# A linear-attention and mixer kernel on one core: own PSUM tiles for the fifth products, and the last outputs on another DMA queue

## The chip, the core and the metric

The kernel runs on one core of a Trainium2 chip. A core has a matrix engine (TensorE, PE), a vector engine (VectorE, DVE), a scalar engine (ScalarE, ACT), a general engine (GpSimd, POOL) and a synchronising engine (SyncE, SP). Each has its own stream of instructions, and they wait for each other through semaphores. PE writes its results into PSUM, from which DVE and ACT read them. Transfers between SBUF and the memory outside are started by SP, ACT or POOL and carried out by 16 DMA engines. The metric is the time of one execution in microseconds (us); lower is better. The kernel before took 264.2 us, the median of three runs (263.92 to 264.7).

## The reference

Eight batches of 576 rows. An attention without softmax makes x of each batch (576 x 512); a mixer over the rows and then one over the channels make the output.

```python
q_p, k_p = (phi(q), phi(k))                       # phi(x) = where(x > 0, x, exp(x) - 1) + 1
kv  = np.einsum('bhsd,bhse->bhde', k_p, v)
z   = np.sum(k_p, axis=2)
num = np.einsum('bhsd,bhde->bhse', q_p, kv)
den = np.einsum('bhsd,bhd->bhs', q_p, z)[..., None] + 1e-06
x   = num / den                                   # heads side by side: 8 x 576 x 512
# ... the mixer
h   = np.maximum(xt @ w_tok1, 0.0) @ w_tok2       # xt: rows and columns of x exchanged
u   = x + h.transpose(0, 2, 1)
h2  = np.maximum(u @ w_ch1, 0.0) @ w_ch2          # 512 -> 1536 -> 512
return (u + h2).astype(np.float32)
```

## The kernel before

The batches are numbered n = 0 to 7 and follow each other in a pipeline. For each batch, `mm3` multiplies u with w_ch1 in 12 tiles (c_ps, line 480), ACT applies the maximum with zero (cr, line 487), and a last product with w_ch2 gives the output. In batches 0 to 5 that last product is done directly (`mm4`, line 506). In batches 6 and 7 it is done by Strassen's scheme in Winograd's form: 512 of the 576 rows and the channels are cut into blocks of two by two, and seven block products take the place of eight. There are two pairs of row tiles, j = 0 and 1, so 14 products of six matmuls each per batch.

```python
ps_big = ctx.enter_context(tc.tile_pool(name="ps_big", bufs=4, space=bass.MemoryType.PSUM))
ps_sm = ctx.enter_context(tc.tile_pool(name="ps_sm", bufs=2, space=bass.MemoryType.PSUM))
outp = ctx.enter_context(tc.tile_pool(name="outp", bufs=5))
# ...
def product(n, j, i):
    b, p = n % 2, n // 2
    a_ = lambda h, e: ablock(n, h, e)[:, :, j]
    lhs, rhs, tile_, first = {
        1: (a_(0, 0), wblock(0, 0), "X", True), 2: (a_(1, 0), wblock(1, 0), "Z", True),
        6: (sb[1][:, :, j], tb[1], "X", False), 5: (sb[0][:, :, j], tb[0], "Y", True),
        7: (sb[2][:, :, j], tb[2], "X", False), 4: (a_(1, 1), tb[3], "X", False),
        3: (sb[3][:, :, j], wblock(1, 1), "Y", False)}[i]
    if first and tile_ != "Y":
        live[tile_, j] = ps_big.tile([128, 512], FP32, name="h2_ps", tag="big")[:, 0:256]
    elif first and j == 0:
        t = ps_sm.tile([128, 2, 512], FP32, name="y_ps", tag="sm")
        live["Y", 0], live["Y", 1] = t[:, 0, 0:256], t[:, 1, 0:256]
    ps = live[tile_, j]
    for k_ in range(KH):                                         # KH = 6; line 606
        nc.tensor.matmul(out=ps, lhsT=lhs[:, k_], rhs=rhs[:, k_], start=(first and k_ == 0),
                         stop=(k_ == KH - 1), skip_group_check=not first)
    if i == 1:
        live["oj", j] = outp.tile([128, 2, DM], FP32, name="o_sb", tag="o_sb")
    o = live["oj", j]
    ur = lambda e, c: u[b][:, 2 * j + e, HC[c]]
    add = lambda e, c, x_, y_: nc.vector.tensor_tensor(out=o[:, e, HC[c]], in0=x_, in1=y_,
                                                       op=ALU.add)   # line 612
    if i == 1:
        add(0, 0, ps, ur(0, 0))
    elif i == 2:
        add(0, 0, ps, o[:, 0, HC[0]])
    elif i == 6:
        add(0, 1, ps, ur(0, 1))
    elif i == 7:
        add(1, 1, ps, ur(1, 1))
        add(1, 1, live["Y", j], o[:, 1, HC[1]])
    elif i == 4:
        add(1, 0, ps, ur(1, 0))
    elif i == 3:
        add(0, 1, ps, o[:, 0, HC[1]])
    if i in (4, 3):
        d, r = (1 if i == 4 else 0), 2 * j + (1 if i == 4 else 0)
        for e in range(2):                                       # line 630
            (nc.scalar if e else nc.sync).dma_start(out=outv[n, :, 2 * r + e],
                                                    in_=o[half[e], d])

ORDER = [(1, 0), (1, 1), (2, 0), (6, 0), (2, 1), (6, 1), (5, 0), (7, 0), (5, 1), (7, 1),
         (4, 0), (3, 0), (4, 1), (3, 1)]                         # (product, j)
```

A product with `first` false goes on adding in PSUM to what the tile holds: X gathers products 1, 6, 7 and 4 of a pair, Y gathers 5 and 3. DVE reads the tile in between, so the same sum serves several output blocks. Products are written (i, j) below. In the profile X and Z are called h_ps (with the numbers in names left out), Y is y_ps, and the output tile is o_sb; the operands of the sums of blocks lie in the space of k_raw, v_raw and q_raw, which the inputs no longer need by then. The row sums that make some of these operands are additions on DVE (line 587).

Each output transfer of batches 6 and 7 carries 64 partitions of 512 fp32 values, 128 KB. The rows that are left over of batches 6 and 7 are the last work of the kernel:

```python
def mm4_last(cs):                   # called with columns 0 to 383, then 384 to 511
    # ... 12 matmuls into h2_ps (line 543), crt x wc2
    o = outp.tile([128, 2, DM], FP32, name="o_sb", tag="o_sb")[:, 0, 0:m]
    nc.vector.tensor_tensor(out=o, in0=ps, in1=ut[p % 2][:, cs], op=ALU.add)      # line 546
    for b in range(2):
        (nc.scalar if b else nc.sync).dma_start(out=outv[2 * p + b, :, 2 * R, cs],
                                                in_=o[half[b]])                   # line 548
```

The outputs of the earlier batches start on GpSimd (`mm4_end`, lines 528 and 535: transfers of 256 KB and of 128 KB). The order of instructions on each engine is the one of the program; the tile framework sets the waits between engines from the tiles that the instructions read and write. The small pool `ps_sm` has two buffers of two banks each; the last tile taken from it ahead of y_ps in batch 6 holds the product that line 284 adds up.

Of the kernel before, what the change touches and what calls it, by code (L numbers as in the profile page):

```python
# [9 lines left out]
FP32 = mybir.dt.float32  # L10
# [8 lines left out]
def kernel(  # L19
# [20 lines left out]
    nc = tc.nc  # L40
# [22 lines left out]
    ps_sm = ctx.enter_context(tc.tile_pool(name="ps_sm", bufs=2, space=bass.MemoryType.PSUM))  # L63
# [32 lines left out]
    half = [slice(0, 64), slice(64, 128)]  # L96
# [22 lines left out]
    live = {}  # L119
# [392 lines left out]
    outv = out.rearrange("n (p t) d -> n p t d", t=T)  # L512
# [52 lines left out]
    def wblock(i, j):  # L565
        return wc2[:, KH * i:KH * (i + 1), 256 * j:256 * (j + 1)]
# [12 lines left out]
    def ablock(n, i, e):  # L579
        return cr[n % 2].rearrange("p k (j e s) -> p k j e s", j=2, e=2)[:, KH * i:KH * (i + 1), :, e]  # L580
# [10 lines left out]
# [7 lines that stand above are left out]
            3: (sb[3][:, :, j], wblock(1, 1), "Y", False)}[i]  # L598
        if first and tile_ != "Y":
            live[tile_, j] = ps_big.tile([128, 512], FP32, name="h2_ps", tag="big")[:, 0:256]  # L600
        elif first and j == 0:
            t = ps_sm.tile([128, 2, 512], FP32, name="y_ps", tag="sm")
            live["Y", 0], live["Y", 1] = t[:, 0, 0:256], t[:, 1, 0:256]
        ps = live[tile_, j]
        for k_ in range(KH):
            nc.tensor.matmul(out=ps, lhsT=lhs[:, k_], rhs=rhs[:, k_], start=(first and k_ == 0),  # L606
# [6 lines that stand above are left out]
                                                           op=ALU.add)  # L613
# [13 lines that stand above are left out]
        if i in (4, 3):  # L627
            d, r = (1 if i == 4 else 0), 2 * j + (1 if i == 4 else 0)
            for e in range(2):
                (nc.scalar if e else nc.sync).dma_start(out=outv[n, :, 2 * r + e],  # L630
                                                        in_=o[half[e], d])

    ORDER = [(1, 0), (1, 1), (2, 0), (6, 0), (2, 1), (6, 1), (5, 0), (7, 0), (5, 1), (7, 1),
             (4, 0), (3, 0), (4, 1), (3, 1)]
# [1 line left out]
    def m4s(n):  # L636
        return [lambda i=i, j=j: product(n, j, i) for i, j in ORDER]
# [128 lines left out]
    def steps(n):  # L766

        out_ = [("kv", lambda: kv(n, range(2)))]
        if n == 1:
            puts = [nc.scalar.copy, nc.vector.tensor_copy if n == 1 else nc.scalar.copy]  # L770
            out_ += [(f"qt{c}", lambda c=c: qtr(n, c, puts[c])) for c in range(2)]
        for i, rs in enumerate(([0, 1], [2, 3], [4])):
            for g in range(2):
                out_.append((f"nd{i}{g}", lambda g=g, rs=rs: nd(n, g, rs)))
        out_.append(("mm1", lambda: mm1(n)))
        if n > 1:
            out_ += [("mm2a", lambda: mm2(n, [0, 1])), ("mm2b", lambda: mm2(n, [2, 3]))]
            if n % 2:
                out_.append(("mm2t", lambda: mm2_tails(n // 2)))
            out_ += [("uta", lambda: utr_dma(n, [0, 1])), ("utb", lambda: utr_dma(n, [2, 3]))]  # L780
            if n % 2:
                out_.append(("utt", lambda: utr_tail_dma(n // 2)))
        return out_
# [34 lines left out]
    first = steps(1)  # L818
# [27 lines left out]
    for n in range(2, B):  # L846
# [11 lines left out]
        if n + 2 < B:  # L858
            d = 1 if n == 2 else 0
# [42 lines left out]
```

## Time and profile before

| what | value |
|---|---|
| time, median of three runs | 264.2 us (263.92 to 264.7) |
| span of the profiled execution | 262.7 us |
| granted TensorE clock | 1.0 of full speed |
| bytes read and written outside | 35.85 MB and 9.44 MB |
| transfers of line 630 | 8 on SP, 8 on ACT, 128 KB each |
| output transfers on POOL | 24 of 256 KB, 6 of 128 KB |

The time of a run is a little longer than the span of the profile, which counts from the first to the last recorded instruction. Times in the text are us from the start of the span. In the groups, a line such as "L606 PE MATMUL y_ps<-wc,v_raw" gives the line of the kernel, the engine, the operation, and what is written from what. In square brackets stands how long the engine sat idle before it, and what released it. A busy PE is not a PE at its peak: matmuls overlap, and their ends are modelled, so two groups that follow each other without a gap can overlap by a little in such a list. PEld is the loading of weights, which runs beside the matmuls. POOLq, SPq and ACTq are the instruction queues of these engines, where transfers are issued. The time to landing of a transfer is counted from its issue to its completion.

### The profile page before, as it was taken

What the parts mean: (1) busy time and instruction counts of PE and PEld (TensorE: products, weight loads), DVE (VectorE), ACT (ScalarE), POOL (GpSimd) and SP (SyncE); (2) the same over time, 40 slices, a digit from 0 to 9 for tenths busy, and PEclk for the clock granted to TensorE, in tenths of its full rate; (3) what the DMA queues carried; (4) which work ended last, traced back from release to release, by engine and by line L of the source; (5) the groups of instructions that cost most, each with busy time, mean ns of one, the idle gap of its engine ahead of it and who ended that gap; (6) DMA issues with size and microseconds to landing.
All of it is one profiled execution on the core that took longest, in us unless ns stands there. A gap on an engine that the chain in (4) does not pass through costs nothing.

```text
span 262.7 us, 5241 instructions
## 1 busy us (share of the span) xinstructions
PE 250.9 (95%) x2126; PEld 138.8 (53%) x2142; DVE 161.8 (62%) x317; ACT 130.8 (50%) x205; POOL 57.6 (22%) x76
## 2 busy tenths in 40 slices
PE   7999999999999999999999999999999999799983
PEld 3674465646644544454644544454644545555962
DVE  5875659866967375847652566748752577714651
ACT  5766763397580659056660669056660652036200
POOL 9750310110011100110012100179819400000000
PEclk9999999999999999999999999999999999999999
DMA  7999999999059952899999953650363404250015
GB/s 261 250 203 274 386 194 390 243 264 410 28 120 228 364 201 38 177 284 406 407 234 250 353 199 60 152 143 0 22 150 81 122 0 41 61 160 2 0 42 160
DMA packets 50088, 48.35 MB, mean 184 GB/s; under 512 B 30288, under 2 KB 35536, under 8 KB 50064
## 3 DMA queue, kind: packets, MB, share of 16 engines
q1 hardware_dynamic: 41824, 35.40, 45.0%
q0 software_dynamic: 7440, 11.44, 20.4%
q10 hardware_dynamic: 800, 1.18, 1.4%
q8 instruction: 17, 0.28, 0.4%
q14 instruction: 7, 0.06, 0.1%
HBM read 35.85 MB, written 9.44 MB: 172 GB/s over the span
## 4 chain that ended last, share of the span: by engine, by line
PE 79%; DMA 8%; DVE 4%; ACT 3%; POOL 3%; issue 1%; SPq 0%; POOLq 0%; DVEq 0%; ACTq 0%
PE c_ps L480 28%; PE h_ps L506 25%; PE a_ps L246 5%; PE c_ps L494 4%; DMA k_raw<-in_k_dram 4%; DMA wc<-in_moe_w_ch_dram 4%; PE h_ps L259 4%; PE nd_ps L208 3%; PE h_ps L606 3%; PE y_ps L606 2%; PE kv_ps L167 2%; DVE o_sb L612 2%; ACT e L124 1%; PE h_ps L543 1%; POOL qT L675 1%
## 5 line engine op out<-in xcount | busy, mean ns | idle before, releaser
L487 ACT ACTIVATE cr<-c_ps 128x512 bf16<-128x512 f32 x91 | 53.2, 599 | 77.6 <-PE c_ps L480 62.7
L480 PE MATMUL c_ps<-uT,wc 128*128 128x512 bf16 x384 | 91.6, 379 | 0.0
L506 PE MATMUL h_ps<-wc,cr 128*128 128x512 bf16 x280 | 65.7, 379 | 0.6
L480 PEld LDWEIGHTS <-wc 128*128 128x128 bf16 x384 | 35.7, 98 | 36.6 <-issue 1.4
L506 PEld LDWEIGHTS <-cr 128*128 128x128 bf16 x288 | 27.5, 98 | 31.8 <-issue 1.2
L528 POOL DMA_DIRECT2D out_dram<-o_sb x24 | 14.5, 609 | 129.9 <-DVE o_sb L523 129.7
L220 DVE TENSOR_TENSOR x<-nd_ps,den 128x512 bf16<-128x512 f32 (+1 forms) x42 | 25.3, 602 | 1.4
L523 DVE TENSOR_TENSOR o_sb<-h_ps,u 128x512 f32<-128x512 f32 x24 | 16.4, 689 | 13.2 <-PE h_ps L506 13.0
L124 ACT ACTIVATE e<-q_raw 128x1152 bf16<-128x1152 f32 x16 | 18.5, 1162 | 6.1 <-DMA q_raw<-in_q_dram 5.9
L124 ACT ACTIVATE e<-k_raw 128x1152 bf16<-128x1152 f32 x16 | 18.7, 1169 | 4.3 <-DMA k_raw<-in_k_dram 4.3
L138 DVE TENSOR_TENSOR qp<-e,y 128x1152 bf16<-128x1152 bf16 x16 | 12.3, 770 | 12.0 <-ACT e L124 11.5
L217 DVE TENSOR_SCALAR den<-nd_ps 128x8 f32<-128x8 f32 (+1 forms) x42 | 6.9, 164 | 19.7 <-PE nd_ps L208 19.0
L271 DVE TENSOR_TENSOR u<-h_ps,x 128x1024 bf16<-128x1024 f32 x12 | 14.7, 1222 | 6.2 <-PE h_ps L259 6.2
L138 DVE TENSOR_TENSOR kp<-e,y 128x1152 bf16<-128x1152 bf16 x16 | 12.1, 757 | 8.0 <-ACT e L124 7.4
L208 PEld LDWEIGHTS <-qT 128*128 128x128 bf16 x140 | 11.4, 98 | 9.3 <-issue 0.2
L208 PE MATMUL nd_ps<-kvbd,qT 128*128 128x130 bf16 x140 | 15.1, 223 | 0.0
L246 PE MATMUL a_ps<-x,w 128*128 128x512 bf16 x50 | 13.9, 379 | 0.3
L149 ACT CAST vs<-v_raw 128x1152 bf16<-128x1152 f32 x12 | 13.9, 1160 | 0.0
L130 DVE TENSOR_SCALAR y<-k_raw 128x1152 bf16<-128x1152 f32 x16 | 12.0, 753 | 2.9 <-DMA k_raw<-in_k_dram 2.8
L130 DVE TENSOR_SCALAR y<-q_raw 128x1152 bf16<-128x1152 f32 x16 | 13.6, 849 | 0.0
L259 PE MATMUL h_ps<-ar,w2p 128*128 128x512 bf16 x48 | 12.3, 379 | 0.0
L606 PEld LDWEIGHTS <-v_raw 128*128 128x128 bf16 x96 | 9.2, 97 | 5.8 <-issue 4.0
(119 smaller groups left out, 275.1 us busy)
## 6 DMA issues: line engine op xcount, KB each, us to landing
k_raw<-in_k_dram SPq DMA_DIRECT2D x16, 576.0 KB, 9.1
q_raw<-in_q_dram SPq DMA_DIRECT2D x16, 576.0 KB, 7.1
v_raw<-in_v_dram SPq DMA_DIRECT2D x14, 576.0 KB, 11.5
out_dram<-o_sb POOLq DMA_DIRECT2D x24, 256.0 KB, 4.9
wc<-in_moe_w_ch_dram POOLq DMA_DIRECT2D x8, 384.0 KB, 10.0
out_dram<-o_sb SPq DMA_DIRECT2D x8, 128.0 KB, 3.0
out_dram<-o_sb ACTq DMA_DIRECT2D x8, 128.0 KB, 3.2
out_dram<-o_sb POOLq DMA_DIRECT2D x6, 128.0 KB, 5.6
```

The lines of the kernel that those rows point to most:

```text
L124: nc.scalar.activation(out=e, in_=f, func=AF.Exp)
L130: nc.vector.tensor_scalar(out=y, in0=f, scalar1=1.0, scalar2=1.0, op0=ALU.add, op1=ALU.max)
L138: nc.vector.tensor_tensor(out=dst.transpose([0, 2, 1, 3]), in0=e.rearrange("p (i t d) -> p i t d", i=nj, t=T), in1=y.rearrange("p (i t d) ...
L208: nc.tensor.matmul(out=o[:, a], lhsT=qT[b][:, t0:t0 + 128], rhs=kvbd[b][:, c, a], start=True, stop=True)
L220: nc.vector.tensor_tensor(out=x[b][:, rs[0]:rs[0] + m, HG * D * g:HG * D * (g + 1)].rearrange("p r (h d) -> p r h d", h=HG), in0=v_[:, :, ...
L246: nc.tensor.matmul(out=ps[:, mt], lhsT=w1t[:, b, ms] if r == R else w1[:, r, ms], rhs=x[b][:, r, :], start=(r == 0), stop=(r == R))
L259: nc.tensor.matmul(out=ps[:, i], lhsT=w2v(kt, r, b), rhs=ar[b][:, kt, :], start=(kt == 0), stop=(kt == NT - 1 and not add))
L480: nc.tensor.matmul(out=ps, lhsT=wc1[:, kj, 128 * mc:128 * mc + 128], rhs=uT[b][:, :, kj], start=(kj == 0), stop=(kj == NDM - 1))
L487: nc.scalar.activation(out=cr[b][:, mc, :], in_=ps, func=AF.Relu)
L506: nc.tensor.matmul(out=ps, lhsT=crt[:, kc, :] if t == 8 else cr[b][:, kc, 128 * r:128 * r + 128], rhs=wc2[:, kc, :], start=(kc == 0), stop ...
L523: nc.vector.tensor_tensor(out=o, in0=ps, in1=u[b][:, r, :], op=ALU.add)
L606: nc.tensor.matmul(out=ps, lhsT=lhs[:, k_], rhs=rhs[:, k_], start=(first and k_ == 0), stop=(k_ == KH - 1), skip_group_check=not first)
```

## The change

The two Y halves of a batch get a PSUM tile each. Before, one tile of two banks held both: the half of j = 0 in the first bank, that of j = 1 in the second. Now each j takes a tile of its own from the same pool and uses its first bank, so a read of one no longer counts as a use of the other. The pool has two buffers, so both are then taken.

The second part moves all 16 output transfers of line 630 from the queues of SP and ACT to that of GpSimd. ACT and SP then have nothing to issue between the products, and their queues hold only the four transfers of `mm4_last` at the end.

```diff
@@ product @@
         if first and tile_ != "Y":
             live[tile_, j] = ps_big.tile([128, 512], FP32, name="h2_ps", tag="big")[:, 0:256]
-        elif first and j == 0:
-            t = ps_sm.tile([128, 2, 512], FP32, name="y_ps", tag="sm")
-            live["Y", 0], live["Y", 1] = t[:, 0, 0:256], t[:, 1, 0:256]
+        elif first:
+            live["Y", j] = ps_sm.tile([128, 2, 512], FP32, name="y_ps", tag="sm")[:, 0, 0:256]
         ps = live[tile_, j]
@@ outputs @@
         if i in (4, 3):
             d, r = (1 if i == 4 else 0), 2 * j + (1 if i == 4 else 0)
             for e in range(2):
-                (nc.scalar if e else nc.sync).dma_start(out=outv[n, :, 2 * r + e],
-                                                        in_=o[half[e], d])
+                nc.gpsimd.dma_start(out=outv[n, :, 2 * r + e], in_=o[half[e], d])
```

## The prediction

> **What bounds the kernel now.** I read the page first (busy times, then the chain), then the waits of the matrix engine alone, then the instructions in order of time through the last stage, then the landing times of the transfers. The page:
>
> ```profile
> PE 250.9 (95%) x2126; PEld 138.8 (53%) x2142; DVE 161.8 (62%) x317; ACT 130.8 (50%) x205; POOL 57.6 (22%) x76
> PE 79%; DMA 8%; DVE 4%; ACT 3%; POOL 3%; issue 1%; SPq 0%; POOLq 0%; DVEq 0%; ACTq 0%
> ```
>
> TensorE is busy for 95% of the span and makes up 79% of the chain that ended last, so an idle gap of PE is lost time almost one for one. DVE's 4% of the chain are links where PE stood still for it. Where? The waits of PE over the whole span, longest first (columns: total us, times, longest us):
>
> ```profile
> PE y_ps L606 <- DVE o_sb L612: 2.6, 4, 1.0
> PE bank L655 <- DVE ones L668: 1.5, 1, 1.5
> PE h_ps L606 <- DVE o_sb L612: 0.5, 1, 0.5
> ```
>
> The largest one is a wait to write y_ps, the tile of products five and three, for the DVE addition that reads it. It occurs four times, twice in each of the last two batches. The last batch in order of time (start, length, engine):
>
> ```profile
> 249.23 0.82 PE L606 MATMUL h_ps<-k_raw,v_raw 128*128 128x256 bf16 x6
> 250.08 0.42 DVE L612 TENSOR_TENSOR o_sb<-h_ps,u 128x256 f32<-128x256 f32 x1 [0.88 <-PE h_ps L606]
> 250.54 0.42 DVE L612 TENSOR_TENSOR o_sb<-y_ps,o_sb 128x256 f32<-128x256 f32 x1
> 251.02 0.81 PE L606 MATMUL y_ps<-k_raw,v_raw 128*128 128x256 bf16 x6 [0.97 <-DVE o_sb L612]
> ...
> 253.47 0.81 PE L606 MATMUL y_ps<-wc,v_raw 128*128 128x256 bf16 x6 [0.32 <-DVE o_sb L612]
> ...
> 255.45 2.78 PE L543 MATMUL h_ps<-wc,crt 128*128 128x384 bf16 x24
> ```
>
> Product (7,0) runs, then DVE adds X and then Y of j = 0. Only after the second addition does (5,1) start, although (5,1) writes the other half of y_ps. The same happens before (3,0), which waits for the addition that reads the half of j = 1.
>
> **What the Trainium skill says.** "PSUM — Partial Sum Buffer", Terms: a bank holds 2 KiB per partition, and what the hardware forbids is two engines on one bank at once. The halves of y_ps start 512 fp32 elements apart, so by that page they lie in two banks and nothing in the hardware asks for this wait; it comes from tracking the tile as one thing. The trace shows the wait and agrees that it is the whole tile that is held. "Perfetto Trace Analysis", Matmuls (under Optimizing Tensor Performance), says that independent matmul groups should rotate through different banks so that the evacuation of one overlaps the next; that is what the new tiles allow. "DMA: Bandwidth & Descriptors", Latency and other measured facts, gives about 1 us to the first byte on GpSimd's path and about 0.6 us on the Sync and Scalar path. The trace has landing times, which I use instead (below), and they point the same way. "SBUF — State Buffer", Who interferes with whom, says that a DVE instruction with one SBUF input outside the two-port modes doesn't contend with GpSimd. The additions here read one operand from PSUM, so I give them their old 0.42 us; no run so far shows them beside such issues.
>
> **Part one, the tiles.** Removed are the four waits; no matmul, addition or byte is added. Undisturbed products start 0.655 us apart (246.61, 247.26, 247.92, 248.57, 249.23 in the order of time). From the start of (7,0) at 249.23 to the first matmul of the last tail at 255.45 are 6.22 us for seven products, which need 7 x 0.655 = 4.59; so 1.63 us are lost. In the batch before, (7,0) starts at 225.39 and the next stage at 231.60: 6.21 - 4.59 = 1.62. Together 3.25 us. This is more than the 2.6 us of the waits view because modelled matmul ends overlap the next product by 0.82 - 0.655 = 0.165 us, and 4 x 0.165 + 2.6 = 3.26.
>
> Does another wait take the place? By the new program, (7,1) waits for the addition of (6,1), (4,0) for X of (7,0), (3,0) for Y of (7,0), (4,1) and (3,1) for those of j = 1. Put (7,0) at t = 0: (5,1) at 0.66, (7,1) at 1.31, (4,0) at 1.97, (3,0) at 2.62, (4,1) at 3.28, (3,1) at 3.93. The additions: X and Y of (7,0) at 0.85 and 1.31, done at 1.75; of (7,1) at 2.15 and 2.61, done at 3.05. Each matmul is later than what it waits for, the closest being (4,0) (1.97 against 1.27) and (4,1) (3.28 against 2.57). DVE has 14 additions of 0.42, 5.9 us, against 14 x 0.655 = 9.2 us of PE. The second tile takes the other buffer of the small pool, whose last reader, the additions of line 284, ends at 224.9; (5,1) would start at 226.05. So I count all 3.25 us. The 0.5 us wait of (7,0) on DVE in the earlier batch stays: there DVE is late with row sums, which the change leaves alone.
>
> **Part two, the queue.** Sixteen transfers of 128 KB leave SP and ACT for GpSimd. For the first eight nobody waits soon. The last eight are close to the end. Landing times (the first line is the pair of 128 KB transfers from GpSimd at 205.6 us, the second the last eight of the old form; then issue on POOL, and the old end):
>
> ```profile
> DMA to landing us min/median/max: 3.7/3.8/4.0
> DMA to landing us min/median/max: 2.3/4.4/4.7
> L535 POOL DMA_DIRECT2D out_dram<-o_sb x2: 539/539/539, 205.6 to 206.2; - x2
> L548 ACTq DMA_DIRECT2D out_dram<-o_sb x2: 474/514/554, 258.5 to 259.6; - x2
> ```
>
> The old end: the last addition is over at 258.56, but the last small transfers go out only at 259.24 on SP (it waited 0.5 us for an earlier output) and 259.56 on ACT. The last lands 2.0 us later, 261.6, and the program closes 1.1 us after that, at 262.7. With the queues of SP and ACT empty, and all of it 3.25 us earlier, these small transfers would be out by about 255.5 and landed by 258.0 (2.0 to 2.8 us).
>
> On GpSimd: product (4,0)'s addition ends at about 251.0 (253.75 before, less the 1.62 of the batch before and the first of this batch's two gaps, 0.97 + 0.165; the second gap comes after it). Eight issues of 0.54 us one after the other go from 251.0 to 255.3, and they set the pace here: a pair needs 1.08 us while products come every 0.655, so GpSimd falls behind and its last issue starts at about 254.8. At 3.7 to 4.0 us to landing that is 258.5 to 258.8. By bytes: 1.31 MB from 252.0 on; GpSimd's earlier outputs ran at about 0.2 MB per us with their start-up (205 to 210 us: 123, 156, 229, 234, 61 GB/s), which gives 258.2 to 258.6, and the receipt after it. I choose 259.1 for the last landing, a little late since the small transfers share the same engines. Plus 1.1 closing: 260.2 to 260.3.
>
> Sum: the span goes from 262.7 to 260.3, 2.4 us less. PE brings 3.25; about 0.85 is given back because GpSimd's queue, not the last addition, now sets the end. 264.2 - 2.4 = 261.8 us.
>
> **Rivals.** (a) The tail eats the gain. For it: the median landing of all six 128 KB transfers from GpSimd is 5.6 us, the longest 7.4, and GpSimd issues serially. With 5.6 the last lands at 260.4, the span is 261.5, the time 263.0; with 7.4 it is 264.8. Against it: those long ones lay beside input loads, and the pair without loads took 3.7 to 4.0. (b) The tail costs nothing: if the eight go out as fast as they are issued, the small HW transfers set the end at about 258.0 + 1.1 = 259.1, and the time is 260.6. This needs landings of about 3 us, which only the fastest of GpSimd's earlier outputs (3.0) showed. (c) The waits remain in another form (DVE slower beside GpSimd's issues, or a PSUM buffer not free): then PE gains 1 us or so and the time is about 264. The working above speaks against it.
>
> **Range and chances.** The centre is 261.8; (b) bounds it below at 260.6, and (a) with the 5.6 us median, above, at 263.0, which I take as 263.1 for the scatter of the measurement (263.92 to 264.7 before). Two per cent are 5.3 us. Even all PE waits and a free tail give 3.6, so faster by over 2% gets 0.02; slower by over 2% would need landings beyond anything here, 0.01; within 2% 0.97.
>
> **What would show it.** Right: no wait of PE y_ps for o_sb; six 0.655 us steps from (7,0) on; the stage of 12 c_ps tiles begins at about 230.0 in place of 231.6, the tail at about 252.2 in place of 255.45; the last GpSimd issue at about 254.8; and the last landing belongs to a transfer of GpSimd, at about 259. Wrong: PE idle in the products still, additions longer than 0.42, or GpSimd transfers landing after 260, in which case the queue and not the tiles decides the result.

## The result, and the profile after

The changed kernel takes 263.95 us, the median of four runs (263.66 to 264.45), beside 264.06 us for the kernel before (four runs as well). The ratio is 0.9994, with a 95% interval from 0.997 to 1.0018: no difference that can be measured, where 2.4 us less were predicted. The span of the profile is 262.1 us, 0.6 less than before.

The waits of the matrix engine in the changed kernel (total us, times, longest us):

```profile
PE bank L653 <- DVE ones L666: 1.5, 1, 1.5
PE bank L178 <- DVE qp L138: 1.3, 1, 1.3
PE h_ps L605 <- DVE o_sb L611: 0.5, 1, 0.5
```

The largest line of before, y_ps waiting for o_sb with 2.6 us, is gone, and the one wait that was to stay (h_ps, 0.5 us) is there. The second line is a wait at 8 us, long before the changed code, which other runs have too, shorter or longer (0.2 us before, 1.4 with the second part alone). Now the last batch in order of time, from product (7,0) to the end of the work on PE and DVE:

```profile
247.82 0.82 PE L605 MATMUL h_ps<-k_raw,v_raw 128*128 128x256 bf16 x6
248.48 0.82 PE L605 MATMUL y_ps<-k_raw,v_raw 128*128 128x256 bf16 x6
...
249.13 0.82 PE L605 MATMUL h_ps<-k_raw,v_raw 128*128 128x256 bf16 x6
...
251.50 4.15 POOL L629 DMA_DIRECT2D out_dram<-o_sb  x8 [18.06 <-DVE o_sb L611]
...
252.41 2.78 PE L543 MATMUL h_ps<-wc,crt 128*128 128x384 bf16 x24
...
254.56 0.96 DVE L546 TENSOR_TENSOR o_sb<-h_ps,ut 128x384 f32<-128x384 f32 x2 [1.52 <-PE h_ps L543]
```

Product (5,1), the second line, follows (7,0) after 0.66 us where it had waited. From (7,0) at 247.82 to the first matmul of line 543 at 252.41 are 4.59 us, where there were 6.22. So the first part did what it was meant to: the last matmuls start 3.04 us earlier (252.41 against 255.45). Counted from the outputs of line 528 at the end of GpSimd's earlier work, which start at 204.41 before and at 204.63 here, the stretch to these matmuls is 3.26 us shorter; 0.22 us were lost ahead of all changed code. But the span is only 0.6 us shorter. Where do the other 2.4 us go? The bytes at the end (stretch, length, then the busy times of PE, PEld, DVE, ACT and POOL, the granted clock, the share of the DMA engines, GB/s):

```profile
257.00:258.00 1.00, 0.00 (x0) 0.00 (x0) 0.00 (x0) 0.00 (x0) 0.00 (x0) 0.96 0.79 227
258.00:259.00 1.00, 0.00 (x0) 0.00 (x0) 0.00 (x0) 0.00 (x0) 0.00 (x0) 0.50 0.39 121
259.00:260.00 1.00, 0.00 (x0) 0.00 (x0) 0.00 (x0) 0.00 (x0) 0.00 (x0) 0.50 0.00 0
260.00:261.00 1.00, 0.00 (x0) 0.00 (x0) 0.00 (x0) 0.00 (x0) 0.00 (x0) 0.50 0.00 0
261.00:262.10 1.10, 0.00 (x0) 0.00 (x0) 0.00 (x0) 0.00 (x0) 0.00 (x0) 0.50 0.00 0
```

From 259 on no byte moves and nothing computes, and yet the program runs for 3.1 us more. What runs there is in the closing instructions of the engines, which all have one line at the end of the file (895 here, 897 before). A DRAIN is an instruction that an engine executes there before it meets the others. The rows for POOL and SP in the changed kernel, then POOL's long one in the kernel before (number of them; shortest, median and longest ns; first and last start):

```profile
L895 POOLq DRAIN  x3: 51/102/6579, 254.8 to 261.9; - x3
L895 SPq DRAIN  x3: 7/7/13, 259.9 to 261.6; - x3
```

```profile
L897 POOLq DRAIN  x1: 6597/6597/6597, 205.2 to 205.2; - x1
```

SP, whose last waits are for output transfers, is through with them at 259.9 (its first drain). POOL's first drain starts at 254.8, while the last transfers are still being issued, and lasts 6.58 us, until 261.4; then the engines meet and the program ends 0.8 us later. Before, a drain of 6.60 us ran from 205.2 to 211.8, because GpSimd had nothing to do after 206.7, and it delayed nobody: the end came 0.8 us after SP was through, at 261.9. The chain that ended last points to the same engine. Its last two pieces in the changed kernel, then the last one in the kernel before:

```profile
254.09 1.04 POOL out_dram L629 x2
255.13 0.52 POOLq L895
```

```profile
258.27 0.29 DVE o_sb L546
```

It ends on GpSimd's queue, where that of the kernel before ended on the last addition of DVE.

This gives **theory A**: the tiles bring their 3 us, and the second part gives them back, because the drain of GpSimd's queue is over only some 5.7 us after its last transfer has been issued (261.4 against 255.65). The rivals are **B**, that it is the landing of GpSimd's transfers that sets the end, and **C**, that the time won on PE is lost somewhere before the end.

### The profile page after: what moved, and what is told of

The parts are those of the page before. It is cut to its first block, busy times and chain, and to the rows that moved or that the text cites. A ratio compares the mean times of both kernels' runs of the same rounds, so it can differ in the third digit from the quotient of the medians.

```text
span 262.1 us, 5249 instructions
## 1 busy us (share of the span) xinstructions
PE 249.9 (95%) x2142; PEld 138.4 (53%) x2142; DVE 161.9 (62%) x317; ACT 131.2 (50%) x205; POOL 65.6 (25%) x92
## 4 chain that ended last, share of the span: by engine, by line
PE 79%; DMA 10%; POOL 3%; DVE 2%; issue 1%; ACT 1%; POOLq 0%; DVEq 0%
PE c_ps L480 28%; PE h_ps L506 26%; DMA wc<-in_moe_w_ch_dram 7%; PE a_ps L246 6%; PE c_ps L494 4%; PE h_ps L259 4%; PE nd_ps L208 3%; PE h_ps L605 3%; DMA cr<-in_v_dram 3%; PE kv_ps L167 2%; PE y_ps L605 1%; POOL out_dram L629 1%; DVE o_sb L611 1%; POOL qT L673 1%; DVE ut L284 1%
## 5 line engine op out<-in xcount | busy, mean ns | idle before, releaser
L528 POOL DMA_DIRECT2D out_dram<-o_sb x24 | 14.5, 608 | 130.8 <-DVE o_sb L523 130.6
L629 POOL DMA_DIRECT2D out_dram<-o_sb x16 | 8.3, 527 | 40.4 <-DVE o_sb L611 40.4
```

## The experiments

The kernels below start from the kernel before or from the changed one. "Tiles alone" is the kernel before with the first part of the change only. Ratios are to the kernel before, run beside them; the intervals are at 95%. An edit that takes out a line with `on_pool` is shown against a version above it that has this line.

### The first part alone

```diff
-        elif first and j == 0:
-            t = ps_sm.tile([128, 2, 512], FP32, name="y_ps", tag="sm")
-            live["Y", 0], live["Y", 1] = t[:, 0, 0:256], t[:, 1, 0:256]
+        elif first:
+            live["Y", j] = ps_sm.tile([128, 2, 512], FP32, name="y_ps", tag="sm")[:, 0, 0:256]
```

> Part one alone: a tile per Y, outputs on SP and ACT as before. Theory A (PE gains what was predicted, and the changed kernel loses it at the end to the drain of GpSimd's queue, 6.6 us long, which starts only after the last transfer issued there): nothing of GpSimd is late here, so the end is 3.2 us earlier than before: span about 259.5, time about 260.9, ratio 0.988. Theory C (the PE waits removed are regained somewhere else before the end, by clock or by another wait): time about 264, ratio 1.0.

Measured: 261.23 us beside 264.35, ratio 0.9878 (0.9859 to 0.9897). The closing instructions of this kernel:

```profile
L896 POOLq DRAIN  x3: 51/93/6618, 205.1 to 258.8; - x3
L896 SPq DRAIN  x3: 7/7/7, 258.3 to 258.6; - x3
```

POOL's drain of 6.6 us is over at 211.7; SP is through at 258.3, and the span is 259.1. Theory C falls: nothing is lost before the end. This version is 1.2% faster than the kernel before, and faster than the changed one, whose interval (0.997 to 1.0018) lies wholly above this one.

### The second part alone

```diff
-                (nc.scalar if e else nc.sync).dma_start(out=outv[n, :, 2 * r + e],
-                                                        in_=o[half[e], d])
+                nc.gpsimd.dma_start(out=outv[n, :, 2 * r + e], in_=o[half[e], d])
```

> Part two alone: one tile for both Y as before, outputs of the last two batches on GpSimd. The PE waits stay. Theory A (drain): last issue at about 257.4, the drain reached at about 257.1, over at 263.7, span about 264.4, time about 265.8 (1.7 slower than before). Theory B (what sets the end is when GpSimd's transfers land): last landing 257.4 + 3.7 = 261.1, span about 262.2, time 263.6, no slower than before.

Measured: 266.68 us beside 264.35, ratio 1.0076 (1.0055 to 1.0097). It is slower, as theory A said, and by more than theory B allows. The last transfer is issued at 257.94 and has landed at 261.74 (3.8 us later); the drain runs from 257.6 to 264.3, and the span is 265.1. SP is through at 262.8, so what SP waits for does not set this end either.

```profile
L896 POOLq DRAIN  x3: 51/93/6649, 257.6 to 264.8; - x3
L896 SPq DRAIN  x3: 7/7/7, 262.8 to 264.5; - x3
```

### Changed kernel, the last batch's outputs back on SP and ACT

```diff
-                nc.gpsimd.dma_start(out=outv[n, :, 2 * r + e], in_=o[half[e], d])
+                on_pool = n == 6
+                (nc.gpsimd if on_pool else nc.scalar if e else nc.sync).dma_start(
+                    out=outv[n, :, 2 * r + e], in_=o[half[e], d])
```

> Changed kernel, but the outputs of the last batch go back to SP and ACT; those of the batch before stay on GpSimd. Theory A: the drain runs from about 233 to 240 under the last batch and is hidden, so the time is that of the tiles alone, about 260.9. Theory C: about 264.

Measured: 261.75 us, ratio 0.9894 (0.9876 to 0.9912), which overlaps that of the tiles alone. The drain runs from 233.2 to 238.4, under the last batch:

```profile
L897 POOLq DRAIN  x3: 51/93/5287, 233.2 to 259.9; - x3
```

The time is 0.85 us above the expected 260.9. In the profile the delay lies ahead of the changed code: the outputs of line 528 start at 205.23, where the tiles alone have 204.32, and from there to the first matmul of line 543 both take 47.77 us. So the eight transfers of the batch before cost nothing that can be seen on GpSimd, and gain nothing there either; the last eight are the ones that count.

### Two of the sixteen transfers less on GpSimd, and four less

```diff
-                on_pool = n == 6
+                on_pool = (n, j, i) != (7, 1, 3)     # 6 of the last batch stay on GpSimd
```

> Changed kernel, but the last two of its 16 transfers, those of product (3,1) of the last batch, go out on SP and ACT. Theory A: GpSimd's last issue ends 1.05 us earlier, so the drain ends 1.05 earlier, at about 260.4, and the time is about 262.9. Theory B: the last landing hardly moves, as the same bytes share the same engines; time 263.6 to 264.

Measured: 263.11 us, ratio 0.9952 (0.9936 to 0.9969). The drain ends at 260.5, 0.88 earlier than in the changed kernel (1.05 were expected), and the span is 261.3, 0.9 less. That is theory A's side.

```profile
L897 POOLq DRAIN  x3: 51/102/6597, 253.9 to 261.0; - x3
L897 SPq DRAIN  x3: 7/7/13, 259.2 to 260.7; - x3
```

```diff
-                on_pool = n == 6
+                on_pool = n == 6 or j == 0           # 4 of the last batch stay on GpSimd
```

> Changed kernel, but of the last batch only the four transfers of the first pair (j = 0) stay on GpSimd; the four of j = 1 go out on SP and ACT. Theory A: last issue on GpSimd ends at about 253.6, drain over at 258.6 to 259.4, span 259.3 to 260.1, time 261.4 to 262.2, which is near the break-even with the tiles alone. Theory B (what counts is bytes and landings, not the drain): no different from the version with six on GpSimd, 263.1.

Measured: 262.13 us, ratio 0.9916 (0.99 to 0.9933). The drain runs from 253.1 to 259.6, the span is 260.4.

```profile
L897 POOLq DRAIN  x3: 51/93/6482, 253.1 to 260.1; - x3
L897 SPq DRAIN  x3: 7/7/7, 259.1 to 259.9; - x3
```

With eight, six and four transfers the drain ends at 261.35, 260.47 and 259.60, and the span is 262.1, 261.3 and 260.4: each time 0.8 us after the drain. The bytes are the same in all three, and from six to four SP is through only 0.1 us earlier (259.2 and 259.1) while the span is 0.9 us shorter. So neither the bytes nor the last landing of all sets the end. GpSimd's own last landing does move with it (258.8, 258.0 and 257.2), but lies 3.2 to 3.3 us ahead of the end, where theory B reckoned with 1.1. In that form theory B falls, with this and with the second part alone; what the landing has to do with the drain comes below.

### What is it that the drain waits for? A late copy, and a late transfer

Both start from the tiles alone, where GpSimd is idle at the end. The expectations call transfers that GpSimd issues software transfers, after the name of its queue in the profile (software_dynamic). First a small copy on GpSimd that waits for the very last addition:

```diff
             (nc.scalar if b else nc.sync).dma_start(out=outv[2 * p + b, :, 2 * R, cs],
                                                     in_=o[half[b]])
+        if cs.start:
+            nc.gpsimd.tensor_copy(out=consts.tile([128, 8], FP32, name="spare", tag="spare"), in_=o[:, 0:8])
```

> Tiles alone (outputs on SP and ACT), plus one small copy on GpSimd (128x8 values of the very last output tile to a spare tile) that waits for the last addition, at about 255.2. Theory A1 (the long drain of GpSimd follows software transfers only): the drain starts after the copy and is short, time as the tiles alone, about 261.2, ratio 0.988. Theory A2 (any late instruction on GpSimd puts the drain of 6.6 us behind it): drain over at about 262, span 262.7, time about 264.8.

Measured: 261.93 us, ratio 0.9912 (0.9896 to 0.9928). Neither theory is right. The copy and the drains:

```profile
255.25 0.19 POOL L551 COPY spare<-o_sb 128x8 f32<-128x8 f32 x1 [48.66 <-DVE o_sb L546]
```

```profile
L898 POOLq DRAIN  x3: 51/93/3972, 255.2 to 259.7; - x3
L898 SPq DRAIN  x3: 7/7/7, 258.5 to 259.5; - x3
```

A copy of 0.19 us is followed by a drain that ends 3.8 us after it, at 259.2, later than SP at 258.5. So the drain is not short after a late instruction that is no transfer, but it isn't 6.6 us either. With no transfer of GpSimd's near, the end is again 0.8 us after the drain (260.0). Then the last transfer of all, 32 KB, on GpSimd:

```diff
-            (nc.scalar if b else nc.sync).dma_start(out=outv[2 * p + b, :, 2 * R, cs],
-                                                    in_=o[half[b]])
+            on_pool = cs.start > 0 and b == 1
+            (nc.gpsimd if on_pool else nc.scalar if b else nc.sync).dma_start(
+                out=outv[2 * p + b, :, 2 * R, cs], in_=o[half[b]])
```

> Tiles alone, but the very last transfer, 32 KB of the last output tile, goes out on GpSimd in place of ACT, at about 255.2. One single late software transfer. Theory A1 (drain long after any software transfer, 5.0 to 5.8 us after the last issue ends, whatever its number): drain over at 260.8 to 261.5, span 261.5 to 262.2, time 263.6 to 264.3. Theory D (the drain is long because eight transfers are outstanding; for one it ends about when that one has landed): span about 259.5, time about 261.6.

Measured: 263.03 us, ratio 0.9949 (0.9931 to 0.9967). The transfer is issued at 256.30, the issue ends at 256.83, it has landed at 258.5, and the drain ends at 260.65: 3.8 us after the issue, 2.1 after the landing.

```profile
256.30 0.53 POOL L549 DMA_DIRECT2D out_dram<-o_sb  x1 [48.87 <-DVE o_sb L546]
```

```profile
L897 POOLq DRAIN  x3: 51/102/4377, 256.3 to 261.2; - x3
```

Theory D falls: the drain goes on well past the landing. Theory A1 is right in that one transfer is enough, but this drain is shorter than it said.

### The number of transfers, or when they land?

In the drains so far, those that ended 3.8 us after the last instruction stood against 5.7 to 5.8 behind the bursts at the end. Three kernels, each run once, narrow down what makes the difference; only the drain is read from them, not the time. Two late transfers:

```diff
-            on_pool = cs.start > 0 and b == 1
+            on_pool = cs.start > 0
```

> Tiles alone, but the last two transfers (32 KB each) go out on GpSimd back to back. So far the drain ended 3.8 us after the end of the last GpSimd instruction for one late copy and for one late transfer, and 5.0 to 5.8 us after it behind four, six or eight transfers. Theory F (any transfer queued behind another adds the extra 1.2 to 2 us once): the drain ends 5.0 to 5.8 us after the last issue. Theory G (the extra grows with the number of transfers in the burst, up to four): it ends about 4.3 us after it. Theory H (the extra has to do with the size, 128 KB against 32 KB): it ends 3.8 us after it.

Measured: the drain ends 3.9 us after the last issue. Four late transfers:

```diff
-            on_pool = cs.start > 0
+            on_pool = True
```

> Tiles alone, but all four transfers of the last rows (two of 96 KB, two of 32 KB) go out on GpSimd, in two pairs 0.5 us or so apart. Theory F and theory G: the drain ends 5.0 to 5.8 us after the last issue. Theory H: 3.8 us after it.

Measured: 4.1 us after the last issue. So two or four transfers give no drain like that of the bursts; theories F and G fall. What is left is size (theory H), or the landing, which took 1.7 to 2.2 us for the last of these small ones and 3.7 to 3.9 us for the last of each burst at the end. One single transfer of 128 KB, among others on SP and ACT:

```diff
-                on_pool = n == 6
+                on_pool = (n, j, i, e) == (7, 1, 3, 1)
```

> Tiles alone, but one single transfer of 128 KB, the second of product (3,1) of the last batch, goes out on GpSimd, at about 252.7, among the others on SP and ACT. Theory K (the drain goes on until about 2.5 us after the last software transfer has landed): with 4 us to landing it has landed at 256.7, and the drain ends at 259.0 to 259.5, some 6 us after the issue's end, although there is only one transfer; span 259.7 to 260.2. Theory F or G (it is the number of transfers in the burst): the drain ends 3.8 us after the issue, at about 257.1, and is hidden; span as the tiles alone, about 259.1 to 259.6.

Measured: it took 4.2 us to land, at 257.4, and the drain ended at 259.3:

```profile
L897 POOLq DRAIN  x3: 51/102/6182, 253.1 to 259.8; - x3
```

That is 5.6 us after the issue's end for one transfer, and 1.9 us after its landing, as theory K said. The size would fit this row as well; it is the other rows with 128 KB that speak against size alone, since their drains ended 4.4, 5.1 and 5.6 to 5.8 us after the issue. All drains together, in us, rounded from the nanoseconds of the records:

| kernel | GpSimd's last issue ends | it has landed | drain ends | after the issue | after the landing |
|---|---|---|---|---|---|
| before | 206.69 | 209.89 | 211.78 | 5.1 | 1.9 |
| changed | 255.65 | 258.81 | 261.35 | 5.7 | 2.5 |
| tiles alone | 206.60 | 209.82 | 211.71 | 5.1 | 1.9 |
| second part alone | 258.47 | 261.74 | 264.28 | 5.8 | 2.5 |
| last batch on SP, ACT | 234.04 | 236.19 | 238.44 | 4.4 | 2.2 |
| six on GpSimd | 254.67 | 258.01 | 260.47 | 5.8 | 2.5 |
| four on GpSimd | 253.84 | 257.23 | 259.60 | 5.8 | 2.4 |
| one of 128 KB | 253.66 | 257.37 | 259.29 | 5.6 | 1.9 |
| one of 32 KB, late | 256.83 | 258.53 | 260.65 | 3.8 | 2.1 |
| two of 32 KB, late | 257.08 | 258.38 | 260.99 | 3.9 | 2.6 |
| four late | 257.34 | 258.56 | 261.42 | 4.1 | 2.9 |
| a copy, no transfer | 255.44 | none | 259.20 | 3.8 | none |

Counted from the issue the drains end 3.8 to 5.8 us later, counted from the landing 1.9 to 2.9. The landing is the better mark, but not an exact one, and the copy shows that some 3.8 us pass with no transfer at all. All rows fit the later of two marks, 3.8 to 4.1 us after the last instruction and 1.9 to 2.5 us after the last landing; that is a fit to these rows and not a cause that was shown. What GpSimd does in that time the records don't show; that stays open.

## Why the prediction was wrong

**PE's gain: right.** 3.25 us were predicted for the tiles. The tiles alone bring 264.35 - 261.23 = 3.12 us, and in the changed kernel the seven products take the 4.59 us that 7 x 0.655 had given. No other wait took the place among the products, so rival (c) fell, and the one of (7,0) in the earlier batch stayed at 0.5 us. The stage after that batch starts at 230.20 (230.0 predicted), the tail at 252.41 (252.2).

**DVE beside GpSimd's issues: right.** The additions at 251.96 and 252.61, during the issues from 251.50 on, take their 0.42 us. That agrees with what the Trainium skill says in "SBUF — State Buffer", Who interferes with whom, of an instruction with one SBUF input.

**The issues and landings on GpSimd: nearly right.** The eight issues run one after the other from 251.50 to 255.65 (251.0 to 255.3 predicted), the last at 255.12 (254.8) with 3.7 us to landing (3.7 to 4.0), at 258.8 (259.1). What was not seen is that the four small transfers on SP and ACT would take 3.6 to 4.1 us to land in place of 2.0 to 2.8. The last landing is therefore one of theirs, at 259.6 on ACT, and not GpSimd's, against one of the signs that were named. They took 3.1 to 3.5 us with six transfers on GpSimd, 2.7 to 3.0 with four and 2.0 to 2.8 with none; why is not shown. SP is through at 259.9; without GpSimd's drain the span would have been about 260.7, an estimate from SP's 259.9 and the 0.8 us that lie between SP and the end in the tiles alone.

The landing times did not "point the same way" as the latencies that the prediction quotes: in its own lines GpSimd's pair took 3.7 to 4.0 us, the eight of SP and ACT 4.4 in the median. The sum does not rest on that sentence.

**"Plus 1.1 closing": wrong, and this is the step that failed.** It took the time from the last landing to the end from the kernel before and carried it over to a kernel whose last transfers are GpSimd's. In the kernel before GpSimd had drained 50 us earlier. In the changed one the end is 3.3 us after GpSimd's last landing (262.1 - 258.8): 2.5 us of drain and 0.8 of closing. Of the miss of 1.8 us in the span (262.1 against 260.3) the drain is some 1.4 us (262.1 - 260.7, with the estimate above), and the slow small transfers and the 0.2 us lost early on are the rest.

**The rival that came nearest** was (a), the tail that eats the gain, but for a wrong reason: it expected long landings of 5.6 to 7.4 us, which gave 263.0 to 264.8. They were 2.9 to 4.0, so that 263.95 lies in between is luck. The sign named for being wrong, GpSimd transfers that land after 260, did not come either. The trace of the kernel before held a hint, the drain of 6.60 us at 205.2 in its closing instructions, which ended 5.1 us after GpSimd's last issue. With the 255.3 predicted for the last issue and 0.8 of closing that would have given an estimate of 261.2 for the span, about half of the miss. The prediction read the landings and the times of SP's last instructions and not the closing instructions of the engine to which the work was moved.

## What to carry to other kernels

Two buffers that are read and written in turn should be two tiles, even where they lie in different banks: here the wait of the whole tile cost 0.8 us at each of four places and came off fully. Before the last transfers of a kernel are moved to another engine, look at how that engine closes: what it does after its last instruction counts as long as it is the last to close. In this kernel GpSimd's last issue would have to end some 6.6 us before the end to cost nothing, an estimate from the longest drain (5.8 us after the issue) and 0.8 of closing. The last outputs are better left to SP and ACT; earlier ones can stay on GpSimd.

## What the runs showed of the hardware

A drain of GpSimd at the end of the program ended 1.9 to 2.9 us after its last transfer had landed, and 3.8 us after a copy of 0.19 us with no transfer; the first drains of SP and ACT in the changed kernel lasted 0.01 and 0.4 us. The profile counts GpSimd's issues as busy (1.00 us from 252 to 253 in the changed kernel) but not its drain (0.00 from 257 on), so the busy times don't show what holds the end.

The mean granted clock of 0.992 in the changed kernel is no loss to the products: the clock is 1.00 up to 257 us, when PE has been through since 255.2, and 0.50 in the empty stretch after 258. An idle time of fixed length after which it falls does not come out of these traces: in the kernel before PE is through at 258.2, and the clock stays at 1.00 until the end, 4.5 us later:

```profile
258.60:262.70 4.10, 0.00 (x0) 0.00 (x0) 0.00 (x0) 0.00 (x0) 0.00 (x0) 1.00 0.38 104
```
